# Sliding-window attention plus token and channel MLP: queries cut into nine blocks of 64, a second copy of v shifted by 64 rows, and value products in column halves

## The chip, the core and the metric

The kernel runs as one program on one core of a Trainium2 chip. The metric is the device time of one execution in microseconds (us). All engines of the core take part: PE (TensorE, matmuls and weight loads), DVE (VectorE), ACT (ScalarE), POOL (GpSimd) and SP (SyncE, which here issues DMAs only). POOL and ACT issue DMAs as well.

## The reference

The inputs are q, k, v of shape (8, 8, 576, 64) (batch, heads, positions, head size), eight global positions, and four weight matrices, all float32.

```python
scores = scale * np.matmul(q, k.transpose(0, 1, 3, 2))
mask = np.abs(pos[:, None] - pos[None, :]) <= 32
mask = mask | is_global[:, None] | is_global[None, :]
attn = softmax(np.where(mask, scores, -1000000000.0))
x = np.matmul(attn, v)                                  # heads side by side: (8, 576, 512)
h = np.maximum(x.transpose(0, 2, 1) @ w_tok1, 0.0) @ w_tok2     # mixes positions
u = x + h.transpose(0, 2, 1)
out = u + np.maximum(u @ w_ch1, 0.0) @ w_ch2                    # mixes channels
```

So a query sees the keys within 32 positions, the eight global keys, and, if it is itself global, all keys.

## The kernel before, in words

Everything is computed in float16 with float32 sums. The kernel is written as functions, each of which issues one step of one batch (`b`), and a long hand-written order that calls them (`manual_schedule`); each engine executes its share strictly in that order.

**Positions.** Keys and values lie in five chunks of 128 rows, shifted by 32 rows: chunk c holds the keys 128c-32 to 128c+95. `vsh` (L73) holds v in this shift, in two buffers that the batches use in turn (`vsh[b % 2]`), each head 66 columns wide: 64 values, a column of ones that yields the sum of the softmax, and a column of zeros. Queries (`qT`, L136) lie transposed in five groups of 144 columns: 8 columns with the global queries, 8 zero columns, 128 queries.

**Scores** (`S_`, L471, called through `S_all`, L528). For one pair of heads p, the two heads sit on partitions 0 to 63 and 64 to 127, so that each matmul uses 64 rows of the array. A chunk of keys is the stationary operand and the queries that can see it stream through: 64 queries to the left of the chunk's diagonal, the 16 extra columns, and 128 queries (208 columns for chunks 1 to 3, 144 for the two ends). This makes ten matmuls per pair of heads (L480), written to two PSUM buffers; three exponentials on ACT (L500, L517, L522) put them into `e_all`, which has 272 columns per head and chunk, with zeros where no query is computed (`e_pads`, L189, six memsets at the start). In batch 0 the mask is added in PSUM by matmuls with the identity (L488). In later batches `SM` (L531) multiplies on DVE: the columns of the global queries into `eg` (L538), and both heads' 5 x 208 columns by the 0/1 mask `bandm` (L544).

**Global queries.** `GK` (L546) and `OG` (L566) compute the global keys' and the global queries' shares; `OG` runs as matmuls with 32 stationary columns (L571), each of four pairs of heads in its own quarter of the array's columns. Their results, `lf` and `rf`, enter the value products as one more product.

**Value products** (`PV`, L582). For each of five groups of 128 queries (`tau`) and each head: a matmul of the queries' scores in chunk tau with `vsh` of chunk tau (L592), and one in chunk tau+1 (L597), both with 128 stationary columns (the queries) and 66 streaming ones. The last group has only L592. Two matmuls with `lf` (L601) finish the PSUM buffer. DVE then takes reciprocals (L608) and scales the result into `x16` or `xl` (L609).

**MLP.** `M1` (L614) and `M2` (L636) mix positions, `M3` (L684) turns the result by DMA transposes on the SP queue, `M4` (L698) and `M5` (L726) mix channels. `M4` and `M5` are the bulk of the matmuls, 128x512 each; the sixty-four rows left over of each batch are done for two batches at once (`M4l`, L712, and the last `M5`).

**The order.** Batch 0's attention is done alone, first. Then `period(b)` (L762) runs the channel MLP of batch b, whose pieces sit in a list (`dense`), interleaved by calls `d(k)` with the attention of batch n = b+1: scores of four pairs of heads (`scores`, L775), GK, OG, five PV with M1 between them, M2, M3. The loads of later batches are placed in between. For batches 3 and later, q and k are turned by DMA transposes on the SP queue (`turns`, L757) and put in order by DVE copies (`order_k` L397, `order_q` L403), some of which stand between the PVs of the batch before.

**DMA queues.** SP issues loads of q and k, DMA transposes and stores of the output, in the order of the program; an instruction there that waits holds up all behind it. POOL issues the weights, v (`load_v16`, L363, a cast from float32 to float16 on the way) and some of the loads of q and k, and casts on POOL stand in the same order. For batch 0, v comes by SP into `lv` and is cast by POOL and DVE (`castv`, L413).

Of the kernel before, what the change touches and what calls it, by code (L numbers as in the profile page):

```python
# [15 lines left out]
P = 128  # L16
# [4 lines left out]
QS = P + GW  # L21
EW = 2 * P + GW
# [4 lines left out]
def kernel(  # L27
# [45 lines left out]
    vsh = [const.tile([P, NT, H, VW], F16, name=f"vsh{i}") for i in range(2)]  # L73

# [36 lines left out]
    e_all = const.tile([P, H, NT, EW], F16)  # L111
# [9 lines left out]
    kp_i = const.tile([P, NT], I32)  # L121
    nc.gpsimd.iota(kp_i, pattern=[[P, NT]], base=-WIN, channel_multiplier=1)
# [16 lines left out]
    def qk_pads(i):  # L139
        nc.gpsimd.memset(kTs[i][:, :, 0:WIN], 0.0)  # L140
        nc.gpsimd.memset(kTs[i][:, :, WIN + S :], 0.0)
        nc.gpsimd.memset(qTs[i][:, :, :, NG:GW], 0.0)
        nc.gpsimd.memset(qTs[i][:, :, NT - 1, GW + LAST :], 0.0)
# [23 lines left out]
    kp_f = to_f("kp_f", kp_i, [P, NT])  # L167
# [20 lines left out]

    def e_pads(i):  # L189
        nc.vector.memset(  # L190
            (
                e_all[:, 2 * i : 2 * i + 2, :, 0:64] if i < NP else e_all[:, :, 0, 64:P] if i == NP
                else e_all[:, :, NT - 1, 64 + GW + P :]
            ), 0.0,
        )
# [45 lines left out]
    band = const.tile([P, 192], F16)  # L241
    nc.gpsimd.memset(band, 0.0)
    left, right = band[:, 0:64], band[:, 64:192]

    nc.gpsimd.affine_select(out=left, in_=left, compare_op=ALU.is_ge, fill=FAR, base=0, pattern=[[1, 64]], channel_multiplier=-1)
    nc.gpsimd.affine_select(out=right, in_=right, compare_op=ALU.is_ge, fill=FAR, base=64, pattern=[[1, P]], channel_multiplier=-1)
    nc.gpsimd.affine_select(out=right, in_=right, compare_op=ALU.is_ge, fill=FAR, base=0, pattern=[[-1, P]], channel_multiplier=1)
# [20 lines left out]

    far = const.tile([P, NT, EW - 64], F16)
    bandm = const.tile([P, NT, EW - 64], F16)  # L270
    rowok = const.tile([P, NT], F32)
# [39 lines left out]
    def masks_a3():  # L311
        ohk = const.tile([P, NT, NG], F32)
        onehot(ohk, kp_f)
        nc.vector.tensor_scalar(out=far[:, :, 72:80], in0=ohk, scalar1=-FAR, scalar2=FAR, op0=ALU.mult, op1=ALU.add)
# [3 lines left out]
        nc.vector.memset(rowok[P - WIN : P, NT - 1 : NT], FAR)  # L318
        nc.vector.tensor_copy(out=far[:, :, 64:72], in_=rowok.unsqueeze(2).to_broadcast([P, NT, NG]))

    def masks_r(c):
        nc.vector.scalar_tensor_tensor(
            out=far[:, c, 80:208], in0=pc["col"][:, P * c : P * c + P], scalar=rowok[:, c : c + 1], in1=right, op0=ALU.add,
            op1=ALU.add,
        )

    def masks_l(c):
        nc.vector.scalar_tensor_tensor(
            out=far[:, c, 0:64], in0=pc["col"][:, P * c - 64 : P * c], scalar=rowok[:, c : c + 1], in1=left, op0=ALU.add,
            op1=ALU.add,  # L330
        )

    def masks_d():
        nc.vector.memset(far[:, 0, 0:64], FAR)
        nc.vector.tensor_scalar(out=bandm, in0=far, scalar1=-1.0, scalar2=None, op0=ALU.is_gt)
# [57 lines left out]
    def order_rest(b):  # L393
        nc.vector.tensor_copy(out=qTs[b % 2][:, :, NT - 1, GW : GW + LAST], in_=rawr[:, :, 0:LAST])
# [8 lines left out]
    def order_q(b, p):  # L403
        nc.vector.tensor_copy(
            out=qTs[b % 2][:, p, 0:4, GW:QS].rearrange("p t (x i) -> p t x i", i=4),
# [7 lines left out]
    def castv(b, cs, copy=nc.gpsimd.tensor_copy):  # L413
        for c in cs:
            r0, r1, _ = vrows(c)
            for a, e in ((WIN, 64), (64, P)) if c == 0 else ((r0, r1),):
                copy(out=vsh[b][a:e, c, :, 0:D], in_=lv[a:e, c])

# [29 lines left out]
    def TE_q(b, p, copy):  # L448
        copy(  # L449
            out=qTs[b % 2][:, p, 0:4, GW:QS].rearrange("p t (x i) -> p t x i", i=4),  # L450
# [13 lines left out]
    def TR(b, copy):  # L464
# [3 lines left out]
        copy(out=qTs[b % 2][:, :, NT - 1, GW : GW + LAST], in_=pr[:, :, 0:LAST])  # L468
        copy(out=kTs[b % 2][:, :, WIN + 512 : WIN + S], in_=pr[:, :, LAST:P])

    def S_(b, p, part):  # L471
        qf = qTs[b % 2][:, p].rearrange("p t x -> p (t x)")
        kT = kTs[b % 2][:, p]

        def score(ps, off, c):
            lo = QS * c - (64 if c else 0)
            n = 64 * (c > 0) + GW + (P if c < NT - 1 else 64)
            for par in range(2):
                r = slice(64 * par, 64 * par + 64)
                nc.tensor.matmul(  # L480
                    ps[:, par, off : off + n], lhsT=kT[r, P * c : P * c + P], rhs=qf[r, lo : lo + n],
                    start=b > 0, stop=b > 0 or c > 1 and c < NT - 1,
                )

        def mask(ps, off, w):
            n = w.shape[1] * (w.shape[2] if len(w.shape) == 3 else 1)
            for par in range(2):
                nc.tensor.matmul(ps[:, par, off : off + n], lhsT=ident, rhs=w, start=off == 0, stop=False)  # L488

        e2 = e_all[:, 2 * p : 2 * p + 2]  # L490
        W = 64 + QS
        ps = pss([P, 2, 512], name=f"s{part}_{b}_{p}")
        if part == 0:
            if b == 0:
                mask(ps, 0, far[:, 1:3, :])
            score(ps, 0, 1)
            score(ps, W, 2)

            def inner():
                nc.scalar.activation(  # L500
                    out=e2[:, :, 1:3, 64:EW], in_=ps[:, :, 0 : 2 * W].rearrange("p h (c x) -> p h c x", c=2),
                    func=AF.Exp, scale=scale,
                )
# [532 lines left out]
```

## Time and profile before

| what | us |
|---|---|
| median of 3 runs (lowest, highest) | 313.11 (312.5, 313.73) |
| the profiled execution, whole | 312.66 |
| its span, first to last instruction | 310.5 |
| PE busy in the span | 299.0 |
| DVE busy in the span | 192.2 |
| ACT busy in the span | 161.8 |
| POOL busy in the span | 78.3 |

The 2.16 us between the span and the whole execution lie before the first and after the last instruction. Busy time of PE is the time in which at least one matmul is under way; matmuls overlap, so the mean duration of a row (379 ns for a 128x512 one) is longer than the distance from one start to the next. Rows are named by the line of the kernel before, for instance L592 for the first value product.

### The profile page before, as it was taken

The numbers are of one execution on the slowest core, as the hardware profiler recorded it, in microseconds if no ns is written. First come the engines' busy times: TensorE is split into PE (matmuls) and PEld (weight loads), VectorE is DVE, ScalarE is ACT, GpSimd is POOL, SyncE is SP. The second block draws the span as 40 slices with busy tenths as digits, with TensorE's granted clock in tenths as the row PEclk, the third lists the DMA queues.
The fourth block names the chain that finished last, engine by engine and source line by source line (L and its number), as shares of the span: only waits on it lengthen the run. The fifth ranks groups of instructions, "written<-read, shape, count | busy, mean of one in ns | idle before, by whom it ended". The sixth has DMA issues, their size and how long they took to land.

```text
span 310.5 us, 6679 instructions
## 1 busy us (share of the span) xinstructions
PE 299.0 (96%) x2672; PEld 159.5 (51%) x2672; DVE 192.2 (62%) x424; ACT 161.8 (52%) x284; POOL 78.3 (25%) x122
## 2 busy tenths in 40 slices
PE   8977999999999999999999999999999999999993
PEld 8554545554565445544574446444574446444641
DVE  7966788679665677567753587667744595520021
ACT  5852795336738564576549383666443283206500
POOL 8887950579831003200230003200000000000000
PEclk9987999999999999999999999999999999999999
DMA  6999999799999999949992699954602410051022
GB/s 208 246 220 270 226 188 298 193 246 197 249 170 128 188 342 179 115 99 274 246 138 36 161 355 120 103 147 122 90 19 51 154 34 2 17 145 59 0 104 68
DMA packets 108513, 48.19 MB, mean 155 GB/s; under 512 B 87106, under 2 KB 102338, under 8 KB 108482
## 3 DMA queue, kind: packets, MB, share of 16 engines
q1 hardware_dynamic: 69712, 33.83, 47.3%
q0 software_dynamic: 38768, 13.93, 42.1%
q8 instruction: 21, 0.34, 0.5%
q14 instruction: 10, 0.08, 0.1%
q10 hardware_dynamic: 2, 0.00, 0.0%
HBM read 36.11 MB, written 9.44 MB: 147 GB/s over the span
## 4 chain that ended last, share of the span: by engine, by line
PE 86%; DVE 10%; ACT 1%; issue 1%
PE op L733 30%; PE b1p L704 25%; PE a1p L624 5%; PE hp L641 4%; PE s L480 4%; PE b1lp L720 3%; PE pv L592 3%; PE pv L601 3%; PE pv L597 3%; DVE e_all L544 2%; DVE qT L449 1%; PE og L571 1%; DVE kT L455 1%; PE idle L892 1%; PE pT L445 1%
## 5 line engine op out<-in xcount | busy, mean ns | idle before, releaser
L704 PE MATMUL b1p<-uT,wc 128*128 128x512 f16 x384 | 94.4, 380 | 1.4 <-DVE b L708 0.6
L733 PE MATMUL op<-wc,b 128*128 128x512 f16 x384 | 88.1, 379 | 0.0
L710 ACT ACTIVATE b<-b1p 128x512 f16<-128x512 f32 x87 | 52.2, 600 | 61.5 <-PE b1p L704 47.5
L733 PEld LDWEIGHTS <-b 128*128 128x128 f16 x384 | 36.1, 98 | 44.1 <-issue 1.6
L704 PEld LDWEIGHTS <-wc 128*128 128x128 f16 x384 | 35.1, 97 | 43.1 <-issue 4.8
L366 POOL DMA_DIRECT2D vsh<-in_v_dram x35 | 30.5, 885 | 96.1 <-PE pv L601 92.2
L737 DVE TENSOR_TENSOR osb<-u,op 128x512 f32<-128x512 f16 x32 | 21.9, 686 | 48.4 <-PE op L733 48.4
L500 ACT ACTIVATE e_all<-s 128x832 f16<-128x832 f32 x32 | 27.6, 862 | 39.3 <-issue 35.2
L544 DVE TENSOR_TENSOR e_all<-e_all,bandm 128x1040 f16<-128x1040 f16 x56 | 37.4, 709 | 1.0
L646 DVE TENSOR_TENSOR u<-x,hp 128x512 f16<-128x512 f16 x28 | 17.4, 682 | 22.6 <-PE hp L641 22.6
L592 PEld LDWEIGHTS <-e_all 128*128 128x128 f16 x320 | 22.0, 100 | 6.4 <-issue 0.9
L592 PE MATMUL pv<-vsh,e_all 128*128 128x66 f16 x320 | 24.5, 197 | 0.0
L609 DVE TENSOR_TENSOR x<-pv,rr 128x512 f16<-128x512 f32 x32 | 22.1, 692 | 1.1
L608 DVE RECIPROCAL rr<-pv 128x8 f32<-128x8 f32 (+1 forms) x40 | 8.3, 206 | 22.7 <-PE pv L601 22.4
L597 PE MATMUL pv<-vsh,e_all 128*128 128x66 f16 x256 | 21.1, 197 | 1.0 <-issue 1.0
L517 ACT ACTIVATE e_all<-s 128x576 f16<-128x576 f32 x32 | 20.8, 648 | 0.0
L597 PEld LDWEIGHTS <-e_all 128*128 128x128 f16 x256 | 17.9, 100 | 3.7 <-issue 0.7
L624 PE MATMUL a1p<-x,w 128*128 128x512 f16 x64 | 19.2, 387 | 0.0
L480 PE MATMUL s<-qT,kT 64*128 64x208 f16 (+1 forms) x320 | 18.8, 241 | 0.0
L480 PEld LDWEIGHTS <-kT 64*128 64x128 f16 x320 | 11.1, 94 | 13.9 <-issue 11.1
L377 ACT CAST qk<-lq 128x512 f16<-128x512 f32 x25 | 15.2, 623 | 5.8 <-DMA lq<-in_q_dram 5.8
L601 PE MATMUL pv<-rf,lf 128*128 128x264 f16 x80 | 16.4, 288 | 0.9 <-DVE rf L576 0.9
(181 smaller groups left out, 354.2 us busy)
## 6 DMA issues: line engine op xcount, KB each, us to landing
out_dram<-osb SPq DMA_DIRECT2D x32, 256.0 KB, 2.3
lq<-in_q_dram SPq DMA_DIRECT2D x4, 1024.0 KB
lk<-in_k_dram SPq DMA_DIRECT2D x4, 1024.0 KB
wc<-in_moe_w_ch_dram POOLq DMA_DIRECT2D x6, 512.0 KB, 9.9
vsh<-in_v_dram POOLq DMA_DIRECT2D x21, 128.0 KB, 6.1
lq<-in_q_dram POOLq DMA_DIRECT2D x2, 1024.0 KB, 9.1
lk<-in_k_dram POOLq DMA_DIRECT2D x2, 1024.0 KB, 12.2
vsh<-in_v_dram POOLq DMA_DIRECT2D x14, 96.0 KB, 7.7
```

Source lines behind the costliest of these rows:

```text
L366: nc.gpsimd.dma_start(out=vsh[b % 2][r0:r1, c, :, 0:D], in_=v[b, :, j0 : j0 + (r1 - r0), :].rearrange("h p d -> p h d"),)
L480: nc.tensor.matmul(ps[:, par, off : off + n], lhsT=kT[r, P * c : P * c + P], rhs=qf[r, lo : lo + n], start=b > 0, stop=b > 0 or c > 1 and ...
L500: nc.scalar.activation(out=e2[:, :, 1:3, 64:EW], in_=ps[:, :, 0 : 2 * W].rearrange("p h (c x) -> p h c x", c=2), func=AF.Exp, scale=scale,)
L544: nc.vector.tensor_mul(out=eh, in0=eh, in1=bandm)
L592: nc.tensor.matmul(o, lhsT=e_all[:, h, tau, EW - P - sh : EW - sh], rhs=vsh[b % 2][:, tau, h, :], start=hh == 0, stop=False,)
L597: nc.tensor.matmul(o, lhsT=e_all[:, h, tau + 1, 0:P], rhs=vsh[b % 2][:, tau + 1, h, :], start=False, stop=False)
L601: nc.tensor.matmul(ps[:, hf, 0 : NP * VW], lhsT=s["lf"][:, P * tau - sh : P * tau - sh + P], rhs=s["rf"][:, 2 * hf : 2 * hf + 2], start=Fa ...
L609: nc.vector.tensor_tensor(out=x_of(b, tau)[r].rearrange("p (f h x) -> p f h x", f=2, h=NP), in0=pq[r, :, :, 0:D], in1=rr[r].unsqueeze(3).t ...
L624: nc.tensor.matmul(ps[tt], lhsT=w, rhs=x_of(b, ch), start=(ch == 0), stop=(ch == NT - 1))
L704: nc.tensor.matmul(ps, lhsT=wc1[:, cc, P * j : P * j + P], rhs=s["uT"][:, cc, :], start=(cc == 0), stop=(cc == 3))
L710: nc.scalar.activation(out=s["b1"][:, j, :], in_=ps, func=AF.Relu)
L733: nc.tensor.matmul(ps, lhsT=w, rhs=wc2[:, j, :], start=(j == 0), stop=(j == NJ - 1))
```

## The change

Queries are handled in nine blocks of 64 (`HB`). Block j needs the 128 keys 64j-32 to 64j+95 and nothing else; these are exactly one chunk of `vsh` for an even j, and for an odd j a chunk of a second copy, `vod`, which is `vsh` shifted by 64 rows. The eight zero columns beside the global queries are gone: a group of queries has 136 columns, and `e_all` has 616 columns per head, with no zero padding.

- Scores: nine blocks, each with 128 keys stationary, 72 streaming columns (even blocks, with the global queries) or 64 (odd blocks), so 18 matmuls per pair of heads; two exponentials (544 and 688 elements per partition) in place of three.
- Masks: `SM` multiplies 616 columns per head instead of 1040, and 80 columns for `eg` instead of 160; the half of `eg` that belongs to the global keys is written once (`key_rows`). Nine `masks_b` of 64 columns replace five `masks_r` of 128 and four `masks_l` of 64. `e_pads` is gone.
- Value products: per head and group of queries two matmuls as before, but each has 64 stationary columns, and the two write to the lower and the upper half of the PSUM partitions. They no longer add into the same rows. In the last group one block is left, and its two `lf` products have 64 stationary columns, too.
- `vod` is filled by `halves`, two copies for each batch that move 64 partitions to the other half: by DVE for batch 0 (four copies), by DMAs on the SP queue for batches 1 and 2, by DMAs on the POOL queue, right behind `load_v16`, for the others. Each DMA moves 64 x 4224 bytes.

```diff
+HB = 64
-QS = P + GW
-EW = 2 * P + GW
+QS = P + NG
+EW = (NT - 1) * QS + NG + HB
...
+    vod = [const.tile([P, NT - 1, H, VW], F16, name=f"vod{i}") for i in range(2)]
...
-    e_all = const.tile([P, H, NT, EW], F16)
+    e_all = const.tile([P, H, EW], F16)
...
+    def masks_b(j):
+        x0 = NG + HB * (j % 2)
+        nc.vector.scalar_tensor_tensor(
+            out=far[:, j // 2, x0 : x0 + HB], in0=pc["col"][:, HB * j : HB * j + HB], scalar=rowok[:, j : j + 1], in1=band,
+            op0=ALU.add, op1=ALU.add,
+        )
...
+    def key_rows(ohk):
+        nc.vector.tensor_copy(
+            out=eg[:, :, :, NG:GW], in_=ohk[:, 0 : 2 * NT - 1 : 2].unsqueeze(2).to_broadcast([P, NT, H, NG])
+        )
...
+    def halves(b, cp, c0=0, c1=NT - 1):
+        v0, v1 = vsh[b % 2], vod[b % 2]
+        cp(out=v1[0:HB, c0:c1], in_=v0[HB:P, c0:c1])
+        cp(out=v1[HB:P, c0:c1], in_=v0[0:HB, c0 + 1 : c1 + 1])
...
     def S_(b, p, part):
         qf = qTs[b % 2][:, p].rearrange("p t x -> p (t x)")
         kT = kTs[b % 2][:, p]
-
-        def score(ps, off, c):
-            lo = QS * c - (64 if c else 0)
-            n = 64 * (c > 0) + GW + (P if c < NT - 1 else 64)
+        e2 = e_all[:, 2 * p : 2 * p + 2]
+        js = range(0, 4) if part == 0 else range(4, 2 * NT - 1)
+        x0, x1 = (0, 2 * QS) if part == 0 else (2 * QS, EW)
+        ps = pss([P, 2, 512], name=f"s{part}_{b}_{p}")
+        if b == 0:
+            for par in range(2):
+                nc.tensor.matmul(ps[:, par, 0 : x1 - x0], lhsT=ident, rhs=farf[:, x0:x1], start=True, stop=False)
+        for j in js:
+            lo, n = QS * (j // 2) + (NG + HB) * (j % 2), HB if j % 2 else NG + HB
             for par in range(2):
                 r = slice(64 * par, 64 * par + 64)
                 nc.tensor.matmul(
-                    ps[:, par, off : off + n], lhsT=kT[r, P * c : P * c + P], rhs=qf[r, lo : lo + n],
-                    start=b > 0, stop=b > 0 or c > 1 and c < NT - 1,
+                    ps[:, par, lo - x0 : lo - x0 + n], lhsT=kT[r, HB * j : HB * j + P], rhs=qf[r, lo : lo + n],
+                    start=b > 0, stop=b > 0 or j == js[-1],
                 )
...
+        def ex():
+            nc.scalar.activation(out=e2[:, :, x0:x1], in_=ps[:, :, 0 : x1 - x0], func=AF.Exp, scale=scale)
...
     def SM(b, p):
...
         for par in range(2):
-            eh = e2[:, par, :, 64:EW]
-            nc.vector.tensor_mul(out=eh, in0=eh, in1=bandm)
+            nc.vector.tensor_mul(out=e2[:, par], in0=e2[:, par], in1=bandm)
...
     def PV(b, tau):
...
         for hf in range(2):
             for hh in range(NP):
                 h = NP * hf + hh
-                o = ps[:, hf, VW * hh : VW * hh + VW]
-                nc.tensor.matmul(
-                    o, lhsT=e_all[:, h, tau, EW - P - sh : EW - sh], rhs=vsh[b % 2][:, tau, h, :],
-                    start=hh == 0, stop=False,
-                )
-                if tau < NT - 1:
+                for i in range(1 if last else 2):
+                    x0, r0 = QS * tau + NG + HB * i, HB * i + sh
                     nc.tensor.matmul(
-                        o, lhsT=e_all[:, h, tau + 1, 0:P], rhs=vsh[b % 2][:, tau + 1, h, :], start=False, stop=False
+                        ps[r0 : r0 + HB, hf, VW * hh : VW * hh + VW], lhsT=e_all[:, h, x0 : x0 + HB],
+                        rhs=(vsh, vod)[i][b % 2][:, tau, h, :], start=hh == 0, stop=False,
                     )
+        r = slice(sh, sh + HB) if last else slice(0, P)
         for hf in range(2):
             nc.tensor.matmul(
-                ps[:, hf, 0 : NP * VW], lhsT=s["lf"][:, P * tau - sh : P * tau - sh + P],
+                ps[r, hf, 0 : NP * VW], lhsT=s["lf"][:, P * tau : P * tau + (HB if last else P)],
                 rhs=s["rf"][:, 2 * hf : 2 * hf + 2], start=False, stop=True,
             )
...
             es = S_all(n, p)
             es[0]()
-            es[1]()
             relu_on_dve[0] = n > 2 and p == 3
             d(1)
             relu_on_dve[0] = False
-            es[2]()
+            es[1]()
...
             masks_d()
             pads(1, nc.vector)
+            halves(1, nc.sync.dma_start)
+        if n == 2:
+            halves(2, nc.sync.dma_start)
         if n > 2:
             load(n + 2)
...
         if 2 < m < B:
             load_v16(m)
+            halves(m, nc.gpsimd.dma_start)
...
-    e_pads(0)
-    e_pads(1)
...
+    key_rows(ohk)
     SM(0, 0)
     SM(0, 1)
...
     castv(0, (1, 2, 3))
+    halves(0, dve, 0, 2)
+    halves(0, dve, 2)
```

More of the change, by code (lines that the diff above doesn't have):

```diff
@@ L267, in pads @@
             eng.memset(xl[LAST:P], 0.0)
[L269 to L271 removed]
+    far = const.tile([P, NT, QS], F16)
+    farf = far.rearrange("p t x -> p (t x)")
+    bandm = const.tile([P, EW], F16)
+    rowok = const.tile([P, 2 * NT - 1], F32)
     mf = const.tile([P, NT * P], F16)
@@ L491, in S_ @@
[L491 to L503, printed above, removed]
-            return [inner]
-        if b == 0:
-            mask(ps, 0, far[:, 0, 64:])
-            mask(ps, QS, far[:, NT - 1, 0:QS])
-            mask(ps, 2 * QS, far[:, 3, :])
```

119 lines of the change are left out of this document (36 added, 83 removed).

## The prediction

> **What bounds the kernel now.** First the page: the busy times and the shares of the chain of work that ended last. Then the busy times by stages (columns: stretch; its length and PE's busy time; PEld, DVE, ACT, POOL; granted clock; DMA share; GB/s).
>
> ```profile
> PE 299.0 (96%) x2672; PEld 159.5 (51%) x2672; DVE 192.2 (62%) x424; ACT 161.8 (52%) x284; POOL 78.3 (25%) x122
> ...
> PE 86%; DVE 10%; ACT 1%; issue 1%
> ```
>
> ```profile
> 35.00:62.00 27.00, 26.12 (x261) 14.01 (x259) 21.14 (x48) 17.20 (x32) 12.09 (x16) 1.00 1.21 223
> 62.00:97.00 35.00, 34.43 (x342) 19.29 (x341) 24.05 (x45) 19.40 (x35) 24.07 (x30) 1.00 1.37 208
> 97.00:131.00 34.00, 34.00 (x279) 16.85 (x277) 24.43 (x52) 19.47 (x35) 4.19 (x5) 1.00 1.69 200
> ```
>
> From 97 us on PE has no gap at all at the full clock: there only PE's own time counts, and what DVE or ACT save is worth nothing. Between 35 and 97 us PE stands still for 0.88 + 0.57 = 1.45 us; DVE's 10% of the chain lies mostly before, in the start. The DMA engines are fully occupied to past 131 us (shares over 1), which matters below: transfers are close behind PE.
>
> **What small and narrow matmuls cost PE.** The chain in order of time (start, length, what) and the timeline of PE (start, length to the last end):
>
> ```profile
> 59.92 1.29 PE op L733 x6
> 62.94 0.55 PE hpl L653 x4
> 63.49 1.40 PE op L733 x6
> 97.87 2.59 PE op L733 x12
> 100.46 0.50 PE s L480 x10
> 100.95 3.99 PE op L733 x18
> ```
>
> ```profile
> 117.63 0.47 PE L571 MATMUL og<-vsh,eg 128*32 128x132 f16 x20
> 118.04 1.04 PE L704 MATMUL b1p<-uT,wc 128*128 128x512 f16 x4
> ...
> 119.02 0.19 PE L592 MATMUL pv<-vsh,e_all 128*128 128x66 f16 x1
> ...
> 119.51 0.39 PE L601 MATMUL pv<-rf,lf 128*128 128x264 f16 x2
> ...
> 126.61 0.42 PE L592 MATMUL pv<-vsh,e_all 128*128 128x66 f16 x8
> 126.86 0.39 PE L601 MATMUL pv<-rf,lf 128*128 128x264 f16 x2
> ```
>
> Twelve 512-column matmuls take 2.59 us, 216 ns each; sixteen of 66 columns with full width take 119.51 - 119.02 = 0.49 us, 30.6 ns each. So a matmul costs about 0.417 ns a column plus 2.5 ns. Then the price of a part of the array: hpl (64 stationary columns) does four 512-column matmuls in 0.55 us where four full ones need 0.86, so the two halves do run side by side; but the six full matmuls behind it take 1.40 instead of 1.29, and its own 0.55 is 0.12 more than two rounds of 216. The same with the scores: behind them eighteen take 3.99 instead of 3.89. **A change between full and part of the array costs 0.10 us each way**, in and out.
>
> **Scores** (nine blocks). They use half the array's rows before and after, so the changes in and out stay. Before, a group streams three pairs of 208 and two of 144 columns: 3 x 89.2 + 2 x 62.5 = 393 ns, which with 0.10 is the 0.50 of the row. After, five pairs of 72 and four of 64: 5 x 32.5 + 4 x 29.2 = 279 ns. That is 0.114 us less, in 28 groups of batches 1 to 7: **-3.2 us**. (Batch 0's four lie in the start, where DVE is last.) More instructions for that, 18 matmuls for 10, cost nothing as long as a pair comes every 29 ns: the value products already get one full matmul in 30.6.
>
> **Value products** (column halves). Now PV leaves full width before its first product and returns for the two `lf` products: 0.20 us that were not there. Sixteen matmuls become eight pairs. What a pair costs no row shows, so it is bounded: 30 ns if the halves overlap fully and weight loads hide; 60 if they don't overlap, which is also what OG's rounds show for 128 loaded columns a round: 118.04 - 117.63 - 0.10 = 0.31 us for five rounds, 62 ns. The nearest rows on weight loads are those of 32 and of 64 columns:
>
> ```profile
> L571 PEld LDWEIGHTS <-eg 128*32 128x32 f16 x160 | 2.6, 96 | 4.4 <-issue 2.5 <-DVE eg L534 1.3 <-DMA lq<-in_q_dram 0.4
> L653 PEld LDWEIGHTS <-w 128*64 128x64 f16 x16 | 0.6, 108 | 1.7 <-issue 1.7
> ```
>
> 32 more columns cost 12 ns, so 64 load in some 24 ns, which a 30 ns matmul covers; I take 33 ns a pair, as it is near its own cover. Then a PV of the first four groups costs 0.20 + 0.024 (the first load, uncovered) + 8 x 0.033 = 0.49 us: **no change**. The fifth group loses: it has eight matmuls in 126.86 - 126.61 = 0.25 us now, and in one half alone no partner, so 0.20 + 0.024 + 0.264 = 0.49, +0.24 in seven batches: **+1.7 us**. Each nanosecond of the pair is worth 35 x 8 = 0.28 us in batches 1 to 7: at 30 ns the sum is 0.8 us lower, at 60 it is 7.6 us higher.
>
> The Trainium skill speaks against the change here: "TensorE: Matmul & The Clock Gate", section "LDWEIGHTS (loading the stationary operand)", puts a load at its columns divided by 1.2 ns, 53 ns for 64, and "TensorEngine Tiling (Array Packing)", section "Restrictions", says that column tiling turns fast weight loading off. By that rule a pair would take 53 ns, 5.6 us more in all; the two rows above don't bear the rate out.
>
> **DVE, ACT and the start.** Group rows of DVE, then the chain at the end of the start, then POOL's casts of v:
>
> ```profile
> L544 DVE TENSOR_TENSOR e_all<-e_all,bandm 128x1040 f16<-128x1040 f16 x56 | 37.4, 709 | 1.0
> L322 DVE SCALAR_TENSOR_TENSOR far<-pcol,rowok,band 128x128 f16<-128x128 f32 x5 | 1.6, 336 | 0.0
> L190 DVE MEMSET e_all<- 128x320 uint32 x4 | 1.3, 325 | 0.1
> L328 DVE SCALAR_TENSOR_TENSOR far<-pcol,rowok,band 128x64 f16<-128x64 f32 x4 | 1.1, 271 | 0.0
> L190 DVE MEMSET e_all<- 128x256 uint32 x2 | 0.5, 272 | 0.0
> ```
>
> ```profile
> 19.16 1.16 PE og L571 x17
> 20.34 0.72 DVE rf L576
> ```
>
> ```profile
> 15.69 1.75 POOL L417 CAST vsh<-lv 128x512 f16<-128x512 f32 x3
> ```
>
> The mask products shrink from 1040 to 616 columns; by columns alone 709 ns becomes 420, at least 0.2 us less for each of 56. DVE gets 11 us or more back, which counts only where PE waits: I let the 1.45 us of waits between 35 and 97 us go: **-1.45**. In the start DVE loses six memsets (1.3 + 0.5) and shortens the masks (5 x 336 + 4 x 271 against 9 x 271 ns: 0.3); it gains the copy of `key_rows` (0.33, like a memset of that size) and four half copies of 1056 columns, some 0.4 each (between 0.3, a memset row, and 0.71, the L544 row). OG could start 1.7 us earlier, not more than 1.6, since POOL casts v to 17.44. The copies, 1.6 us, stand between OG and `rf`, partly while OG waits and runs. I take **-1.2** for the start, between 0 and -1.9. ACT's saved exponentials (its share of the chain is 1%) count nothing.
>
> So far -3.2 + 1.7 - 1.45 - 1.2 = -4.15 us.
>
> **The copies by DMA.** What queues where (issues with landing times in us; SP's and DVE's timeline):
>
> ```profile
> 35.29 3.60 POOL L366 DMA_DIRECT2D vsh<-in_v_dram  x4
> ```
>
> ```profile
> vsh<-in_v_dram POOLq DMA_DIRECT2D x1, 96.0 KB, 7.7
> ```
>
> ```profile
> 52.79 0.19 PE L592 MATMUL pv<-vsh,e_all 128*128 128x66 f16 x1
> ```
>
> ```profile
> out_dram<-osb SPq DMA_DIRECT2D x32, 256.0 KB, 2.3
> ```
>
> ```profile
> lr<-in_q_dram SPq DMA_DIRECT2D x1, 128.0 KB, 6.4
> ```
>
> ```profile
> 76.81 16.36 SPq L391 DMA_TRANSPOSE raw<-qk  x8
> ```
>
> ```profile
> raw<-qk SPq DMA_TRANSPOSE x8, 11.9
> ```
>
> ```profile
> 92.15 0.76 DVE L398 COPY kT<-raw 128x512 f16<-128x512 f16 x1
> ```
>
> Batch 1: the last chunk of v is issued at about 37.9 and lands 7.7 later, near 45.6. Only then can SP's two copies start; they take between 2.3 us (the stores) and 6.4 (a load on SP, asked for between 51 and 52 us, in the same crowd), and the second is issued half a microsecond after the first: `vod` is there at 48.4 to 52.5. PV(1,0) starts at 52.79 now; earlier by 1.2, by the 0.88 of waits and by 0.45 of scores it would want it at 50.3. Batch 2: SP holds its two copies until the v of batch 2 has landed, and two stores and the nine DMA transposes of batch 3 stand behind them. Those transposes take 11.9 us in the median: one issued at 78, the second in SP's row, lands near 90, and DVE's copy of the first k begins at 92.15, among the work of batch 2's last PV; behind it DVE owes PE the results of M5 and M2. From batch 3 on POOL waits for v instead and has nothing urgent behind it, and v lands tens of microseconds ahead. I charge **+1.15** for the two places, between 0 and the 3.1 us gained by then.
>
> The sum is -3.0 us. The profiled execution took 312.66, so 309.7; the median of the runs shown, 313.11, lies 0.45 above it, so **310.1** for a median.
>
> **The rivals.**
> 1. *The pairs of halves are slower than a pair is worth* (weight loads of 64 columns, or halves that take turns). For it: no row shows narrow matmuls in halves, and OG's 62 ns a round can be read as 128 columns being loaded. Against it: hpl's halves overlap, and 24 ns of load. At 44 ns the sum is zero, from there on the change is slower. At 60 ns PE loses 7.6 us and the DMA waits disappear behind it: -4.15 + 7.6 = +3.4, 316.5; at 53, the skill's figure, +1.45, 314.6.
> 2. *The copies by DMA take the place of the waits that went.* All that is gained before 97 us, 1.2 + 1.45 + two sevenths of 1.5 = 3.1 us, is waited away at PV(1,0) and at the order of batch 3; what is left is five batches of PE, -1.1: 312.0. For it: the crowded queues and the 2 us between a transpose's landing and its use; against it: few large pieces, 4224 bytes each. The skill's "DMA: Bandwidth & Descriptors", section "Queues, rings and completion order", lets each engine go round the queues packet by packet, so that SP's copies needn't wait for POOL's megabytes; that would favour the next case.
> 3. *No DMA wait at all* and 30 ns a pair: -4.15 - 0.8 = -5.0, 308.1; with the start at its best, 307.4.
>
> **How the numbers follow.** Forecast 0.42, rival 1 0.25, rival 2 0.18, rival 3 0.15. The range goes from 307.4 to rival 1's end, 316.5, with 0.6 us on either side for the spread of the runs (312.5 to 313.73): 306.8 to 317.1. A difference under 0.5% (1.6 us) can't be told from none here. Faster: nine tenths of the forecast, rival 3, a sixth of rival 2: 0.56. Slower: rival 1 and a third of rival 2: 0.30. The rest, 0.14, is no change.
>
> **What would show it.** A group of scores in the chain at 0.39 instead of 0.50; sixteen value products in 0.27 us between two changes of 0.10; the fifth group's eight in the same time; memsets gone and `rf` near 19 us; PE's gaps between 35 and 97 us at PV(1,0) and after 90 us behind a DMA, under 1.5 us in all. The forecast is wrong if a pair takes over 44 ns, if a narrow group costs more than 0.10 to enter or leave, or if PE waits over 4 us for `vod` or for the transposes of batch 3.

## The result, and the profile after

| kernel | median, us | lowest to highest | runs |
|---|---|---|---|
| before | 313.21 | 312.5 to 313.73 | 4 |
| changed | 328.91 | 327.75 to 330.65 | 4 |

The changed kernel is slower by 5.1%: ratio 1.0508, 95% interval 1.0456 to 1.0559. The profiled execution took 328.9 us (span 327.1) against 312.66. Rows of the changed kernel bear its own lines: L483 scores, L507 mask products, L556 value products, L562 the products with `lf`, L584 `M1`, L601 `M2`, L664 `M4`, L693 `M5`, L359 `load_v16`, L378 and L384 the DMA transposes, L414 and L415 the two copies of `halves`.

The page of the changed kernel, busy times and the chain of work that ended last:

```profile
PE 300.0 (92%) x2912; PEld 150.5 (46%) x2912; DVE 179.9 (55%) x421; ACT 145.4 (44%) x252; POOL 82.4 (25%) x129
...
PE 72%; DMA 14%; DVE 8%; ACT 2%; issue 1%; SPq 1%; ACTq 0%
```

DVE and ACT did lose work (12 and 16 us), PE's busy time is nearly the same (300.0 us against 299.0), and DMAs, which had no share in the chain before, hold 14% of it. Where, the stretches tell (length and PE's busy time; PEld, DVE, ACT, POOL; granted clock; DMA share; GB/s):

```profile
35.00:62.00 27.00, 19.82 (x234) 10.03 (x231) 15.73 (x39) 13.56 (x25) 9.79 (x14) 0.90 1.28 223
62.00:97.00 35.00, 35.00 (x355) 17.22 (x355) 22.39 (x45) 13.82 (x24) 21.95 (x29) 0.98 0.97 200
97.00:131.00 34.00, 30.67 (x302) 15.70 (x302) 19.19 (x44) 17.85 (x31) 7.17 (x10) 1.00 1.50 192
131.00:165.00 34.00, 28.78 (x233) 12.62 (x231) 17.58 (x39) 14.96 (x28) 4.50 (x6) 0.90 1.19 184
165.00:201.00 36.00, 35.87 (x354) 18.01 (x353) 20.28 (x45) 18.51 (x34) 5.76 (x7) 1.00 1.10 201
```

PE stands still for 7.2 us between 35 and 62 us, where before it was 0.88, and for 3.3 and 5.2 us in the two stretches between 97 and 165, where before it had no gap at all; and in the two stretches with the long standstills the granted clock is 0.90. From 165 us on PE works with hardly a gap again. The first `M2` matmul of each batch dates the loss (start in us before, and how much later it starts in the changed kernel):

| batch | 0 | 1 | 2 | 3 | 4 | 5 | 6 | 7 |
|---|---|---|---|---|---|---|---|---|
| before | 30.61 | 61.05 | 95.98 | 130.15 | 164.94 | 199.00 | 233.80 | 267.86 |
| changed | -0.81 | +7.45 | +7.79 | +17.01 | +17.09 | +16.84 | +16.61 | +16.37 |

So there are two delays, 8.3 us within batch 1 and 9.2 us between batches 2 and 3, and then 0.24 us a batch are won back. The chain in these places (start, length, what):

```profile
46.72 11.26 DMA vod<-vsh
...
58.02 0.65 PE pv L556 x15
```

```profile
86.18 14.60 DMA rawr<-rn
...
100.80 0.23 DVE qT L387
...
102.04 0.59 PE a1p L584 x2
```

```profile
126.24 10.85 DMA rawr<-rn
...
137.63 0.70 DVE x L569
...
138.37 1.01 PE a1p L584 x2
```

In the first, PE waits at PV of batch 1 until the second copy of `vod` has landed, 11.26 us after its issue. In the others a DMA transpose of the next batch (`rawr`) lands late; DVE's copy out of it stands ahead of the scaling of a value product (`x`, `xl`) in DVE's order, and `M1` waits for that, 1.2 us near 101 us and 5.2 us near 133. Another 1.7 us PE waits near 119 us, at `M4`.

In the steady part the chain shows what the change does on PE:

```profile
200.13 0.38 PE s L483 x18
...
206.24 0.38 PE pv L556 x16
206.61 0.33 PE pv L562 x2
...
208.24 0.38 PE pv L556 x16
...
212.25 0.37 PE pv L556 x8
212.62 0.23 PE pv L562 x2
212.84 0.54 PE a1p L584 x2
```

and of the kernel before:

```profile
190.75 0.86 PE b1p L704 x4
...
192.76 0.86 PE b1p L704 x4
...
195.62 0.26 PE pv L592 x8
195.88 0.23 PE pv L601 x2
196.10 0.43 PE a1p L624 x2
```

A group of scores takes 0.38 us instead of 0.50. A step of PV, `M1` and `M4` takes 208.24 - 206.24 = 2.00 us; the same step took 192.76 - 190.75 = 2.01 before. The fifth group takes 0.37 + 0.23 + 0.54 = 1.14 us to the end of `M1`, where it took 0.26 + 0.23 + 0.43 = 0.92.

### The profile page after: what moved, and what is told of

Its sections match the earlier page's. It is cut to its first block, busy times and chain, and to the rows that moved or that the text cites. A ratio compares the mean times of both kernels' runs of the same rounds, so it can differ in the third digit from the quotient of the medians.

```text
span 327.1 us, 7128 instructions
## 1 busy us (share of the span) xinstructions
PE 300.0 (92%) x2912; PEld 150.5 (46%) x2912; DVE 179.9 (55%) x421; ACT 145.4 (44%) x252; POOL 82.4 (25%) x129
## 4 chain that ended last, share of the span: by engine, by line
PE 72%; DMA 14%; DVE 8%; ACT 2%; issue 1%; SPq 1%; ACTq 0%
PE op L693 29%; PE b1p L664 16%; DMA rawr<-rn 10%; PE a1p L584 5%; PE hp L601 4%; PE pv L556 4%; DMA vod<-vsh 3%; PE pv L562 3%; PE s L483 3%; PE b1lp L680 2%; PE pT L443 1%; PE idle L855 1%; DVE e_all L507 1%; ACT e_all L489 1%; PE hpl L613 1%
## 5 line engine op out<-in xcount | busy, mean ns | idle before, releaser
L664 PE MATMUL b1p<-uT,wc 128*128 128x512 f16 x384 | 95.0, 382 | 2.2 <-DVE eg L505 1.7
L693 PE MATMUL op<-wc,b 128*128 128x512 f16 x384 | 88.1, 379 | 0.0
L489 ACT ACTIVATE e_all<-s 128x544 f16<-128x544 f32 x64 | 41.9, 692 | 43.4 <-issue 37.4
L693 PEld LDWEIGHTS <-b 128*128 128x128 f16 x384 | 36.1, 98 | 43.0 <-issue 1.6
L664 PEld LDWEIGHTS <-wc 128*128 128x128 f16 x384 | 35.2, 98 | 42.8 <-issue 6.3
L359 POOL DMA_DIRECT2D vsh<-in_v_dram x35 | 30.2, 879 | 68.3 <-PE pv L556 63.4
L556 PEld LDWEIGHTS <-e_all 128*64 128x64 f16 x576 | 15.1, 121 | 24.7 <-issue 16.6
L507 DVE TENSOR_TENSOR e_all<-e_all,bandm 128x616 f16<-128x616 f16 x56 | 25.4, 494 | 1.0
L584 PE MATMUL a1p<-x,w 128*128 128x512 f16 x64 | 20.4, 408 | 5.4 <-DVE x L569 5.2
L556 PE MATMUL pv<-vod,e_all 128*64 128x66 f16 x256 | 15.9, 210 | 6.7 <-DMA vod<-vsh 6.3
L370 ACT CAST qk<-lq 128x512 f16<-128x512 f32 x25 | 15.1, 619 | 11.0 <-DMA lq<-in_q_dram 6.4
L556 PE MATMUL pv<-vsh,e_all 128*64 128x66 f16 x320 | 19.9, 208 | 0.0
L562 PE MATMUL pv<-rf,lf 128*128 128x264 f16 (+1 forms) x80 | 17.6, 306 | 1.5 <-DVE rf L539 1.5
L483 PEld LDWEIGHTS <-kT 64*128 64x128 f16 x576 | 11.1, 95 | 15.0 <-issue 13.1
L483 PE MATMUL s<-qT,kT 64*128 64x72 f16 (+1 forms) x576 | 15.5, 193 | 0.9 <-ACT e_all L489 0.4
L391 DVE COPY kT<-raw 128x512 f16<-128x512 f16 x20 | 12.2, 608 | 4.3 <-DMA raw<-qk 4.3
L370 ACT CAST qk<-lk 128x512 f16<-128x512 f32 x21 | 12.9, 620 | 2.6 <-DMA raw<-qk 2.3
## 6 DMA issues: line engine op xcount, KB each, us to landing
lq<-in_q_dram POOLq DMA_DIRECT2D x2, 1024.0 KB, 11.2
```

What stands on the lines that cost most here:

```text
L359: nc.gpsimd.dma_start(out=vsh[b % 2][r0:r1, c, :, 0:D], in_=v[b, :, j0 : j0 + (r1 - r0), :].rearrange("h p d -> p h d"),)
L370: eng(out=qk[:, ti, p].rearrange("q i (r d) -> q r i d", r=2), in_=(lq, lk)[ti][:, hs])
L483: nc.tensor.matmul(ps[:, par, lo - x0 : lo - x0 + n], lhsT=kT[r, HB * j : HB * j + P], rhs=qf[r, lo : lo + n], start=b > 0, stop=b > 0 or ...
L489: nc.scalar.activation(out=e2[:, :, x0:x1], in_=ps[:, :, 0 : x1 - x0], func=AF.Exp, scale=scale)
L507: nc.vector.tensor_mul(out=e2[:, par], in0=e2[:, par], in1=bandm)
L556: nc.tensor.matmul(ps[r0 : r0 + HB, hf, VW * hh : VW * hh + VW], lhsT=e_all[:, h, x0 : x0 + HB], rhs=(vsh, vod)[i][b % 2][:, tau, h, :], s ...
```

## The experiments

Two theories. **D**: the copies of `vod` by DMA cost the time, by landing late and by disturbing the queues; what the change does to PE is the small gain that the steady part shows. **P**: the narrow products and new blocks cost PE the time, and the waits only take the blame. All runs in one table: how much later `M2` of a batch starts than in the profile of before, the time, and, where both kernels were timed several times side by side, the ratio to the kernel before. A kernel without a ratio ran once. The columns of batches come from one profiled execution each; that of e12, 317.52 us, was the fastest of its six.

| run | copies of batch 1; 2; 3 to 7 | b. 0 | b. 1 | b. 2 | b. 3 | b. 7 | us | ratio (95%) |
|---|---|---|---|---|---|---|---|---|
| changed | SP; SP; POOL queue | -0.8 | +7.5 | +7.8 | +17.0 | +16.4 | 328.91 | 1.0508 (1.0456, 1.0559) |
| e11 | none | -0.7 | +0.2 | +0.7 | +0.4 | -0.5 | 311.67 | 0.9948 (0.9907, 0.9988) |
| e1 | DVE | +0.9 | +1.3 | +1.1 | +2.0 | +5.5 | 317.8 | 1.0163 (1.0100, 1.0225) |
| e2 | SP; DVE; DVE | +1.0 | +7.8 | +7.6 | +8.5 | +12.0 | 324.66 | |
| e3 | DVE; SP; DVE | -0.5 | +0.1 | -0.9 | +0.2 | +3.8 | 315.99 | |
| e4 | DVE; DVE; POOL queue | +0.7 | +1.1 | +1.8 | +8.4 | +7.5 | 320.20 | |
| e6 | as e4, issued later | 0.0 | +0.8 | +1.5 | +8.6 | +7.9 | 320.63 | |
| e9 | as e15 | +0.2 | +0.6 | +1.3 | +1.0 | +0.1 | 312.45 | |
| e15 | as e4, behind the next v | -0.3 | +0.7 | +2.2 | +2.0 | +1.1 | 313.09 | 1.0038 (1.0012, 1.0065) |
| e12 | DVE; SP; behind the next v | +0.6 | +0.5 | +0.6 | +6.2 | +5.3 | 320.35 | 1.0246 (1.0201, 1.0291) |
| e13 | DVE; SP; POOL queue | -0.7 | +1.2 | +1.8 | +10.7 | +9.8 | 322.32 | |
| e14 | SP; SP; behind the next v | +0.9 | +9.6 | +9.2 | +16.5 | +15.6 | 328.09 | |
| e8 | as changed, PE kept busy | +1.8 | +7.7 | +7.8 | +18.1 | +17.9 | 330.40 | |
| e7 | loads from memory | -0.9 | +1.9 | +7.1 | +15.9 | +15.0 | 327.39 | |
| e5 | POOL; DVE; POOL | +0.6 | +0.7 | +3.3 | +4.2 | +3.2 | 314.70 | 1.0050 (1.0019, 1.0080) |
| e10 | POOL; DVE; DVE early | +1.6 | +2.8 | +3.4 | +3.2 | +2.3 | 314.72 | 1.0045 (1.0009, 1.0082) |

The start (batch 0) differs by 2.7 us among kernels that hardly differ there; steps between batches of one run tell more than sums.

**Without the copies (e11).** Only the DMAs of batches 1 to 7 are gone; the odd blocks of these batches multiply batch 0's `vod`, so that the result is another one.

```diff
-            halves(1, nc.sync.dma_start)
...
-            halves(2, nc.sync.dma_start)
...
-            halves(m, nc.gpsimd.dma_start)
...
-                        rhs=(vsh, vod)[i][b % 2][:, tau, h, :], start=hh == 0, stop=False,
+                        rhs=(vsh[b % 2], vod[0])[i][:, tau, h, :], start=hh == 0, stop=False,
```

> The changed kernel with the copies of batches 1 to 7 left out: the odd blocks of those batches multiply batch 0's vod, so their v is another one; every instruction of PE, DVE and ACT stays. What the change is worth without the price of the copies. By the prediction's terms (scores -3.2, fifth group +1.7, waits -1.45, start -1.2 to +1): 308.5 to 311.5 us. If the narrow products cost PE more than that: over 313.

Measured: 311.67, just above the expected range, and half a per cent faster than before. Both delays are gone and P with them: all of PE's new instructions are in this kernel. From batch 2 to 7 it gains 0.23 to 0.24 us a batch. But the waits between 35 and 97 us have not become shorter. Its stretches there, what PE waited for, and a piece of its chain:

```profile
35.00:62.00 27.00, 25.01 (x286) 12.47 (x285) 20.24 (x47) 14.72 (x26) 11.91 (x17) 1.00 1.25 227
62.00:97.00 35.00, 33.69 (x372) 17.91 (x371) 22.64 (x45) 16.50 (x30) 23.81 (x31) 1.00 1.51 206
```

```profile
PE pg L344 <- DVE g_q L338: 1.4, 1, 1.4
PE b1p L664 <- DMA uT<-u: 1.3, 1, 1.3
PE b1p L664 <- DVE b L668: 0.5, 1, 0.5
```

```profile
67.14 7.32 DMA uT<-u
```

DVE is still the last to arrive in two places: 1.4 us for the copy `g_q`, which took 2.6 us here and 0.6 before, where PE did not wait for it, and 0.5 us for a relu `b`, where it was 0.6. In the third place, where PE had waited 0.4 us for DVE, `M4` of batch 1 now waits for the DMA transposes of its own input: the last of them was 7.3 us under way, 5.2 before.

**The copies on DVE (e1), and one batch group at a time by DMA (e2, e3, e4).** In e1 the three DMA lines are gone, and behind `GK(n)` stands

```diff
+        halves(n, dve, 0, 2)
+        halves(n, dve, 2)
```

e2, e3 and e4 each leave one of the three DMA lines in its place.

> All copies into vod of batches 1 to 7 are made by DVE (four of 64x1056 elements each, behind GK of the batch) instead of DMAs; all else is as in the changed kernel. Theory D (the DMA copies cost the time: the rows of M2 fall 7.5 us behind the kernel before by batch 1, another 9.2 us between batches 2 and 3, and gain 0.23 us a batch from then on): both delays go, 310 to 313.5 us (the profiled 312.66, + 1.0 for the later start that stays, - 1.6 for seven batches at 0.23, - 1.45 for the waits of 35 to 97 us, + 0 to 2 where PE waits for the added 1.9 us of DVE a batch). Rival P (the narrow products or the new blocks cost PE the time, the waits for DMAs only take the blame): the waits for vod and rawr go, but the time stays over 322.

> Only batch 1's two copies are DMAs on SP, as in the changed kernel; DVE makes those of batches 2 to 7. Theory D: the wait at PV of batch 1 is back (6.5 us) with a stretch of half clock behind it, the second delay isn't: the run above + 6 to 8 us. If the first delay also causes the second (everything later by 7 us, the queues in step no more), + 12 to 16. Rival P: no change against the run above.

> Only batch 2's two copies are DMAs on SP, ahead of two stores and the nine transposes of batch 3. Theory D: SP waits for v of batch 2, the transposes of batch 3 are issued behind POOL's loads of q and k of batch 4, and land 10 us or more later than their issue; PE waits 1 to 4 us near 92 to 100 us: the first run + 1 to 4. If the transposes get through in 4 to 5 us as in the kernel before, + 0 to 0.5.

> Only the copies of batches 3 to 7 are DMAs, on POOL's queue right behind the loads of v. Theory D: POOL waits for v of batch 3 with batch 4's load behind it, those loads fall among the loads of q and k of batch 5, and rawr of batch 4 lands late: PE waits about 5 us near 120 to 135 us and the clock halves for 6.8 us behind it: the first run + 5 to 9. If POOL's queue can wait without harm, as the prediction had it (nothing urgent behind it), + 0 to 0.5.

e1 has no delay left, but misses its 310 to 313.5: it loses 0.9 us a batch from batch 3 on to a wait that DVE's copies bring with them. Its chain:

```profile
220.57 0.43 DVE vod L415
...
221.03 0.49 DVE lf L527
221.53 0.61 DVE b L668
...
222.18 1.02 PE b1p L664 x4
```

A relu on `M4`'s result (`b`, L668), which this order gives to DVE during the last scores, stands behind the copies, and the next `M4` waits for its PSUM buffer.

e2 brings the first delay back: batch 1 takes 6.8 us longer than before, and no second delay follows from it. e4 brings the second: 6.6 us between batches 2 and 3. e3 costs nothing, against the expectation. So the first delay is the two copies on SP for batch 1: it is there in every run with them (changed, e2, e8, e14) and in none of those that fill batch 1 on DVE. For e4, POOL's timeline and the chain:

```profile
99.25 0.54 POOL L414 DMA_DIRECT2D vod<-vsh  x1 [15.22 <-DMA vsh<-in_v_dram]
...
100.38 4.23 POOL L359 DMA_DIRECT2D vsh<-in_v_dram  x5
```

```profile
117.17 10.52 DMA rawr<-rn
...
127.71 0.23 DVE qT L387
```

POOL stands 15.2 us at the copy of batch 3, until v of batch 3 has landed; the load of v of batch 4, which before was issued at 84 to 96 us, is issued at 100 to 104, a few microseconds ahead of q and k of batch 5, and `rawr` of batch 4 comes behind all of them.

**Whether it is the place in POOL's queue (e6, e9, e15).**

> DVE copies for batches 1 and 2, DMAs on POOL for 3 to 7 as before, same bytes, but issued in the next batch, ahead of the scores, when v has long landed, so that POOL waits for nothing and v of the next batch is loaded on time. If the blocked queue made the second delay: it goes, M2 of batch 3 stands 1 to 2.5 us behind the kernel before instead of 8.4, then 0.23 us less with each batch, 313 to 315.5 in all. If the traffic of the copies made it: 318 to 321, as with the copies issued behind the loads (320.2).

e6 issues the copies a batch later in the program, and nothing changes. It did not test what it was to test: POOL is a batch ahead of the others, still waited 15.5 us at the copy of batch 3, and its next instruction behind the copies was still the load of the next v (at 100.3 us). e9 (and e15, the same kernel, run twelve times) moves the load ahead of the copies:

```diff
+            if m < B:
+                load_v16(m)
+            halves(n, nc.gpsimd.dma_start)
         scores(0, tail > 5)
```

> DVE copies for batches 1 and 2; the DMAs of batches 3 to 7 on POOL stand one load of v further back: those of batch 3 behind the load of batch 4, so that POOL's wait for v of batch 3 holds up no load. In the run with the DMAs ahead of the scores they still stood ahead of that load, and v of batch 4 was issued at 100 to 104 us instead of 84 to 97. In the run with copies on POOL, too, the load was that late (104 to 108 us), and rawr of batch 4 came in time. So two accounts are left. If the late load is needed for the second delay: M2 of batch 3 stands 1.5 to 3 us behind the kernel before, 313 to 315.5 us in all. If the copies' own traffic (264 KB each, four of them between 99 and 114 us) suffices: M2 of batch 3 stands 6 us or more behind, 317 to 320.5.

> The same kernel as the one look at 312.45 us (DVE copies for batches 1 and 2, DMAs for 3 to 7 behind the load of the next v), timed in rounds. If that look was typical: 311.5 to 314, a ratio of 0.995 to 1.003. If the order of the queues there hangs on a microsecond: a median over 315 with runs several us apart.

e9 took 312.45 us, e15 313.09. POOL's timeline of e15 and its stretch:

```profile
97.70 0.78 POOL L359 DMA_DIRECT2D vsh<-in_v_dram  x1 [3.98 <-DMA vsh<-in_v_dram]
101.23 0.54 POOL L414 DMA_DIRECT2D vod<-vsh  x1 [2.75 <-DMA vsh<-in_v_dram]
```

```profile
97.00:131.00 34.00, 34.00 (x313) 15.86 (x310) 22.94 (x52) 17.57 (x32) 7.13 (x10) 1.00 1.69 208
```

The kernel moves the same bytes in all, and PE has no gap. So this delay is made by the place of the copies in POOL's row. By which of two ways the runs don't separate, as e15 moved two things: the load of v of batch 4 is issued to its end by 97.7 us (104 in e4), and the copies of batch 4, which e4 issued at 110.4 and 111.7, ahead of `rawr` of batch 4 (117.2), come at 130. The late load alone isn't enough: in e5 below v of batch 4 was issued at 104 to 108 us, and `rawr` landed after 7.0 us.

**Whether that is all of the second delay (e12, e13, e14).** e12 was to be the best of all: DVE for batch 1, SP for batch 2 as in e3, POOL's copies behind the load as in e15. e13 is the changed kernel with DVE for batch 1. e14 is the changed kernel with POOL's copies behind the load.

> What did no harm in the runs, together: batch 1's copies by DVE, two behind GK and two behind the last scores of the batch; batch 2's by DMAs on SP; those of batches 3 to 7 by DMAs on POOL behind the load of the next v. If the delays were only where the earlier runs put them, M2 of batch 2 stands 0 to 1 us ahead of the kernel before as in the run with batch 2's DMAs alone, each later batch gains 0.23 us, and the time is 310 to 312 us, a ratio of 0.990 to 0.997 to the kernel before, at the level of the run without copies (0.9948). If the three pieces disturb one another (SP's copies late, then rawr of batch 3, then the loads behind it), 314 or more.

> The changed kernel with batch 1's copies by DVE; those of batch 2 on SP and of batches 3 to 7 on POOL right behind their load, as in the change. If the delays add up, M2 of batch 1 stands about 1 us behind the kernel before and that of batch 3 some 8 to 10 us: 320 to 323 us. If the second delay needs the 7 us of the first (the queues out of step): M2 of batch 3 stands under 4 us behind, 314 to 317.

> The changed kernel with one thing moved: the copies of batches 3 to 7 stand in POOL's queue behind the load of the next v. The first delay stays (M2 of batch 1 7.5 us behind). If the place in POOL's queue made the second: M2 of batch 3 stands 7 to 9 us behind, 319.5 to 322 us. If SP's copies of batch 2, which put rawr of batch 3 behind POOL's loads of q and k, make it just as well: M2 of batch 3 stands 12 to 17 us behind, 324 to 329 us.

e12 failed by 8 us, and e14 still has a second delay of 7.3. SP's copies alone made none (e3), nor did POOL's behind the load of the next v (e15); the two together do. The timeline of SP in e12 and its chain:

```profile
76.43 0.54 SPq L414 DMA_DIRECT2D vod<-vsh  x1
77.20 0.92 SPq L415 DMA_DIRECT2D vod<-vsh  x1
78.21 1.30 SPq L698 DMA_DIRECT2D out_dram<-osb  x2
79.60 2.41 SPq L378 DMA_TRANSPOSE rawr<-rn  x1
```

```profile
79.60 14.02 DMA rawr<-rn
...
93.64 0.23 DVE qT L387
```

SP waits for v of batch 2, then issues the copies and two stores, and `rawr` of batch 3 goes out at 79.60 instead of 75.49. In those 4 us POOL has issued q of batch 4 (1 MB, at 78.98). Its landing goes with this order in all seventeen traces: where `rawr` of batch 3 went out ahead of that load (eleven) it landed after 4.2 to 7.9 us; in the five in which SP's copies for batch 2 had put it behind (changed, e8, e12, e13, e14) it took 11.6 to 14.6, and 11.2 in e3, and in these six it landed 0.7 to 2.0 us behind POOL's load of k of batch 4. SP's copies stand ahead of `rawr` in all six as well; in e12 they had landed by 81.2 us, 12 us before it. In e3 no wait of PE followed that e1 doesn't have. In e12 and e14, where POOL's copies of batch 3 go out at 100 to 112 us, PE waits at what stands behind `rawr` in SP's row: 4.1 us at the scores of batch 3 in e14, for their transposes,

```profile
108.07 9.02 DMA raw<-qk
...
118.36 0.47 PE s L483 x10
```

and in e12 2.5 us at these scores, 1.7 for `uT` and 1.2 behind `rawr` of batch 4. That POOL's copies tip it is inferred from e3 and e12, each with one profile. e13, with the first delay gone, has the second one in full (9.0 us): the second doesn't need the first.

**The half clock (e8).** Thirty matmuls more, which leave no trace in the result, ahead of PV of batch 1:

```diff
+        if b == 1 and tau == 0:
+            for _ in range(30):
+                nc.tensor.matmul(ps[:, 0], lhsT=ident, rhs=wc1[:, 0, 0:512], start=True, stop=True)
```

> The changed kernel with 30 added 128x512 matmuls (6.5 us at full clock) ahead of the first value product of batch 1, into the same PSUM buffer, which the real products then overwrite. PE works while vod is on its way, and is done with them about when vod lands. If the half clock of 56.9 to 63.7 us is a consequence of the 6.5 us standstill, it goes, and the time falls by 1.5 to 3 us against the changed kernel, to 326 to 327.5; if not, it stays at 328 to 331.

The first stretch of e8:

```profile
35.00:62.00 27.00, 26.03 (x275) 13.39 (x275) 15.54 (x40) 15.67 (x29) 9.40 (x14) 1.00 1.22 210
```

The clock stays at 1.00, where it was 0.90. What that is worth, the work from the first real value product of batch 1 to `M2` tells; first e8, then the changed kernel:

```profile
60.51:68.79 8.28, 8.26 (x105) 4.35 (x105) 5.20 (x12) 1.51 (x2) 6.03 (x8) 1.00 0.84 268
```

```profile
58.02:68.50 10.48, 10.48 (x103) 5.36 (x104) 5.39 (x12) 2.46 (x4) 6.19 (x8) 0.73 0.81 241
```

In the kernel before it took 8.26 us (52.79 to 61.05). So 2.2 us of the first delay are the half clock behind the wait, not the wait; in e2 and e14 the same work took 9.6 and 10.8 us, 1.3 and 2.5 too many. The whole of e8 was not faster, against the expectation: the added matmuls ended 2.3 us after `vod` had landed (58.2 us), the start was 2.6 us later in this execution, and the second delay was 10.4 us long.

**Other ways to fill `vod` (e7, e5, e10).**

> vod is loaded from v in memory by four more DMAs a batch on POOL right behind those of vsh (1 MB read each time), with no copy and no wait for vsh; its columns of ones and zeros are set once. Batch 1's vod then lands behind four more chunks, each some 0.75 us behind the last as the chunks of vsh do: near 49.5 us, in time for PV of batch 1. If the wait for one transfer to end before the next can start is what cost the time: 311 to 315. If the crowd on the DMA engines is: the added megabytes push q and k of batches 2 to 4 and the transposes back, 318 or more.

> As the run with all copies on DVE, but the copies are moved to where their engine waits for nothing: POOL makes those of batch 1 (ahead of its casts of k of batch 2; it stood still 11.4 us there) and of batches 3 to 7 (a batch ahead, in its standstill of over 20 us), DVE those of batch 2, and in batch 0 ACT makes two and DVE the other two behind rf. Theory D with the prediction's sums for PE: the 1.2 us that PE waited in each of the batches 3 to 7 for the relu behind DVE's copies go (PE then gains 0.23 us a batch), the later start goes too: 308.5 to 311 us. If copies on POOL are in the way there too (of its loads, or of DVE): 312 to 315.

> No DMA copies. POOL copies for batch 1, DVE for batch 2 behind GK, as in the run with copies on POOL; for batches 3 to 7 DVE copies early, two ahead of the scores and two behind those of the first pair of heads, where it waits some 2 us for M5 each time; in batch 0 DVE copies chunk 0, ACT chunks 2 and 3, DVE chunk 1 behind rf. DVE's copies of q and k took 1.2 to 1.46 us instead of 0.6 beside POOL's copies, and the relu behind DVE's late copies held PE 1.2 us; both are avoided here. If all that is left is the change on PE, it gains 0.23 us a batch from batch 3 on, and the sum is 309.5 to 312, a ratio of 0.993 to 1.000; if DVE's 1.9 us a batch are in the way wherever they stand, 314 to 318.

e7 reads v twice from memory and so waits for nothing; batch 1 loses 2.7 us instead of 8.3, but the added megabytes push all else back by 5.2 us in batch 2 and 8.8 in batch 3. e5 and e10 have no DMA copies. e5 shows a new price, in its timeline of DVE:

```profile
114.41 1.24 DVE L391 COPY kT<-raw 128x512 f16<-128x512 f16 x1
115.58 1.46 DVE L397 COPY qT<-raw 128x512 f16<-128x512 f16 x1
```

The median of these copies is 0.60 us; here POOL copies `vod` at the same time. e10 avoids that and loses nothing from batch 3 on (it gains 0.23 us a batch), but it loses 1.2 us in batch 1 and 0.6 in batch 2, and its start was late. No version that computes everything was shown to beat the kernel before; e15 comes closest, at 1.0038.

## Why the prediction was wrong

The direction was wrong, and the time lies 12 us above the range. By the prediction's own steps:

- **Scores, -0.114 us a group: right.** 0.50 became 0.38.
- **Value products, no change, and +0.24 for the fifth group: right.** 2.01 became 2.00, and 0.92 became 1.14. Pairs of halves start every 32 ns in the trace at full clock, 33 were taken. Rival 1 is out, and with it the 53 ns that the Trainium skill's "TensorE: Matmul & The Clock Gate", section "LDWEIGHTS (loading the stationary operand)", led to. The change between full and part of the array at 0.10 us each way holds, too: the two products with `lf` take 0.33 us instead of 0.23, with the way back in them.
- **DVE's waits, -1.45: wrong.** Without any copies (e11) PE still stands 27.00 - 25.01 + 35.00 - 33.69 = 3.3 us between 35 and 97 us: 1.9 for DVE, which had less to do in all but was no earlier in these two places, and 1.3 for the transposes `uT`, 7.3 us under way. The step took DVE's saved time for time saved where PE waits, and didn't ask what is late next.
- **The start, -1.2, with `rf` near 19 us: not settled.** `rf` started at 21.39, later than before, since all four copies stand ahead of it on DVE; batch 0 was done 0.8 us earlier all the same. With starts that differ by 2.7 us from one execution to the next, one profile of each can't tell.
- **The copies by DMA, +1.15, at most 3.1: this is the step that failed.** Against e11 they cost 17 us. What the step rested on fell in four places:
  - `vod` of batch 1 was put at 48.4 to 52.5 us, from landings of 2.3 to 6.4 us. The two copies took 8.5 and 11.3 us and were there at 58.0, beside q and k of batch 2 (1 MB each) in POOL's queue.
  - The step's bound, and rival 2, held that waits for DMAs can only eat the 3.1 us gained before 97 us. They weren't bounded by that: one came to 6.3 us, one to 5.2. Rival 2 had the cause right and the size wrong.
  - The price of a standstill was taken to be its length. Behind the first one 2.2 us of half clock come on top.
  - POOL was said to have "nothing urgent behind it". Behind its wait stood the next load of v and, behind that, the next copies, which fell into the time of q, k and the transposes of the batch after (e4 against e15). And the stores and transposes behind SP's wait were seen, but priced by their use 2 us after landing, not by the place in line that they would lose (e12).

The sum without that step was -4.15 us; e11, the kernel without copies, measures -1.6 by its ratio (interval -2.9 to -0.4), which is what the two terms of PE alone give (7 x 0.24 less 28 x 0.114 = -1.5). "PE waits over 4 us for `vod` or for the transposes of batch 3" was named as what would make the forecast wrong; it was that, with batch 4's transposes in place of batch 3's for the larger wait. How much of the 9.2 us belongs to SP's copies and how much to POOL's stays open: POOL's ahead of the next v make 6.6 and 7.2 us without SP's (e4, e6), POOL's behind it make 5.6 and 7.3 with SP's (e12, e14) and none without them (e15), so the shares don't add. That SP's copies in e3 did no harm rests on a single execution.

The sentence in the prediction after the Trainium skill's "DMA: Bandwidth & Descriptors", section "Queues, rings and completion order", that turns taken packet by packet would spare SP's transfers, is not borne out where they go out behind megabytes: 11.2 to 14.6 us against 4.2 to 7.9.

## What to carry to other kernels

Where the DMA engines are full, price a new transfer by what it makes late, not by its own length: list what stands behind it and behind its wait in the same queue, and ask which of these has a place ahead of a large load that it would lose. That a queue runs far ahead of the other engines doesn't mean that it has slack to wait in: here its wait delayed a load that was due a batch later. And time that is gained on an engine counts only up to the next thing that is late at the same place, be it a DMA, as `uT` here, or the same engine with another instruction.

## What the runs showed of the hardware

- A standstill of PE can cost more than itself: within those of 6.3 and 5.2 us of the changed kernel the granted clock fell to 0.50, for 6.83 us each time (from 56.9 and 135.4 us), and pairs of value products behind the first took 54 ns instead of 32. The Trainium skill's "TensorE: Matmul & The Clock Gate", section "HAM oscillation — how this bites in real kernels", says that PE must not idle for more than some 3.4 us; both standstills were longer, and in e8, where the added matmuls filled the first, the clock stayed at 1.00. Shorter ones were not always free, though: those of 1.95 us in e5 (from 75.0 us) and 1.97 us in e13 (from 112.7) were followed by 3.41 us at 0.50, those of 2.4 and 2.5 us in e10 and e12 were not.
- DVE's 128x512 copies took 1.24 and 1.46 us instead of 0.60 while POOL copied, and two of its mask operations in e5 took 1.9 us instead of 0.2 and 0.5 while POOL cast.
- A 264 KB copy from SBUF to SBUF landed after 3.0 us in the changed kernel behind 140 us, after 8.5 and 11.3 beside two megabyte loads, and after 15.1 at the longest (e14).
- One DMA transpose, `rawr` of batch 3, landed after 4.2 to 7.9 us where it was issued ahead of POOL's megabyte loads of q and k, and after 11.2 to 14.6 where it was issued behind that of q.
